# Seven block products for eight in half of the last batch's first product

## Chip, cores and metric

One core of a Trainium2 chip. The metric is the device time of one execution in microseconds (us). The engines are TensorE (PE, with its weight loads PEld), VectorE (DVE), ScalarE (ACT), GpSimd (POOL) and SyncE (SP, which here issues DMAs). Each runs its own queue in order; an instruction that waits holds up those behind it on its engine.

## The reference

Two stages: a cross attention between x (8 batches, 8 heads, 512 rows, 64 columns) and a state of 32 rows, and a two-layer product with a leaky ReLU on the result, 544 rows a batch (512 of x, 32 of state).

```python
scores = scale * x @ state.T          # softmax over the 32 state rows
xread = softmax(scores) @ state
scores2 = scale * state @ x.T         # softmax over the 512 rows of x
sread = softmax(scores2) @ x
t = concatenate([xread, sread], axis=2)   # heads side by side: (4352, 512)
h = t @ w_in                          # (4352, 2048)
g = maximum(0.01 * h, h)
out = g @ w_out                       # (4352, 512)
```

## The kernel before

Everything is computed transposed and in bf16 with fp32 sums. For the x rows of a batch the attention read and the first product are joined: `a.M` (2 halves of 128 rows, 2048 columns) is state times w_in, `a.aT` (2 halves of 128 rows, 512 columns) the softmax. `ff1` (L369) computes one block j of 128 of the 2048 columns of h: two matmuls of 512 columns (L372), one for each half g, into a PSUM tile `ph` of which there are two, and a leaky ReLU on ACT (L377) into `hT[:, j, :]`.

The second product of batches 2 to 7 is done by `Batch` and `Fast` with the Strassen-Winograd scheme: hT and w_out are cut into 2 x 2 blocks and multiplied in seven block products, numbered 1, 2, 6, 5, 7, 3, 4 in their order, each of eight units m (`Fast.unit`, L557: two matmuls of 256 columns). It needs sums of hT blocks (`Fast.sums`, L546, on DVE), sums of w_out made once, and it alternates between two PSUM banks: products 1, 6, 7, 4 add up in one, 2, 5, 3 in the other. Between products the bank is copied or joined: ACT copies 1, 6, 5 and 7 (`save`, L566), POOL adds 7 to 5 (L627), DVE joins 2, 3 and 4 with a copy and so makes the output (L569), and SP stores it (L594).

The loop over b from 2 (L932) has 16 steps s for each batch. Step s does `ff1` for j = s, small work of the attention of the next batch, and then `fill(s)`: `PACE[s]` units of second products, first those left of the batch before (41 of them), then the batch's own first 15. Batch 7 has no next batch (`nxt is None`), so its steps hold instead: at s=1 the last block of M, at s=4 the first three sums of w_in blocks for the sread rows (`FastIn.w_sum` 0, 1, 2, L411, each 128x2048 on DVE), at s=8 batch 7's sread (L300, L307), at s=10 the fourth (`w_sum(3)`) and the four sums of sread columns (`x_sums`, L423), at s=12 sums of hT for its own second product.

After the loop the sread rows of all batches (256 columns) go through both products: `FastIn.product` (L425) is a Strassen-Winograd product of w_in with them, seven products for each of two halves r in four PSUM banks, with copies on ACT (L463) and DVE (L465), joins on DVE (L468), an addition on POOL (L471) and leaky ReLUs on ACT (L457). Units of batch 7's second product run between. The schedule is manual: each engine's queue has the order in which the program issues its instructions. Tile pools with a tag and a number of buffers set the waits: a new tile of a tag waits for the last reader of the buffer that it takes.

Of the kernel before, what the change touches and what calls it, by code (L numbers as in the profile page):

```python
# [9 lines left out]
P = 128  # L10
B, H, S, D = 8, 8, 512, 64
# [8 lines left out]
BF16 = mybir.dt.bfloat16  # L20
FP32 = mybir.dt.float32
AF = mybir.ActivationFunctionType
ALU = mybir.AluOpType
# [4 lines left out]
def kernel(  # L28
# [9 lines left out]
    nc = tc.nc  # L38
# [4 lines left out]
    att = ctx.enter_context(tc.tile_pool(name="att", bufs=2))  # L43
# [4 lines left out]
    psum = ctx.enter_context(tc.tile_pool(name="psum", bufs=2, space=bass.MemoryType.PSUM))  # L48
# [5 lines left out]
    VEC, SCA, POO = nc.vector.tensor_copy, nc.scalar.copy, nc.gpsimd.tensor_copy  # L54
# [40 lines left out]
    xs, xl = {}, {}  # L95
# [273 lines left out]
    def ff1(a, hT, j):  # L369
        ph = psum.tile([P, S], FP32, name="ph", tag="ph")  # L370
        for g in range(2):
            nc.tensor.matmul(  # L372
                ph[:], lhsT=a.M[:, g, P * j:P * (j + 1)],
                rhs=a.aT[:, g, :],
                start=(g == 0), stop=(g == 1),
            )
        nc.scalar.activation(out=hT[:, j, :], in_=ph[:], func=AF.Prelu, alpha=0.01)  # L377
# [12 lines left out]
    class FastIn:  # L390


        R = NK

        def __init__(self, hT):
            w = w_in_bf[:].rearrange("p (r k) (i f) -> p i r k f", r=2, i=2)
            self.W = {(i, r): w[:, i - 1, r - 1] for i in (1, 2) for r in (1, 2)}
            x = sr_t[:].rearrange("p (c b) (r k) n -> p r c k b n", r=2, c=2)
            self.X = {(r, c): x[:, r - 1, c - 1] for r in (1, 2) for c in (1, 2)}
            self.hT, self.S, self.T = hT, {}, {}  # L400
            self.bank, self.sv = [{}, {}], [None, None]
# [23 lines left out]
        def product(self, r, n):  # L425
            b = self.bank[r]
            if n in (1, 2):
                tag = ("ph", "ph") if r == 0 else ("big", "sc")
                b[n] = psum.tile([P, self.R, P], FP32, name="pf", tag=tag[n - 1], bufs=2 - r)[:]
            bank = b[n] = b[{1: 1, 6: 1, 7: 1, 4: 1, 2: 2, 5: 2, 3: 2}[n]]  # L430
            W, X = self.W, self.X
            lhs = {1: W[1, 1], 2: W[1, 2], 4: W[2, 2]}.get(n)
            if lhs is None:
                lhs = self.S[{3: 3, 5: 0, 6: 1, 7: 2}[n]]
            rhs = {1: X[1, 1], 2: X[2, 1], 3: X[2, 2]}.get(n)
            if rhs is None:
                rhs = self.T[{4: 3, 5: 0, 6: 1, 7: 2}[n]]
            for q in range(self.R):
                j = self.R * r + q
                for k in range(2):  # L440
                    nc.tensor.matmul(  # L441
                        bank[:, q, :], lhsT=lhs[:, k, P * j:P * (j + 1)], rhs=rhs[:, k],
                        start=(n in (1, 2, 5) and q == 0 and k == 0), stop=(k == 1),
                        skip_group_check=True,
                    )
            self.done(r, n, bank)

        def done(self, r, n, bank):
# [23 lines left out]
            elif n == 4:  # L472
                relu(1, 1, sv[5])
                relu(1, 0, flat)

    class Y:
        pass

# [46 lines left out]
    class Fast:  # L525
# [9 lines left out]
        def sums(self, n, m0=0, m1=NM, eng=None):  # L535
            A, S = self.A, self.S
            if n not in S:
                pool, tag, bufs = self.homes[n]
                S[n] = pool.tile([P, NM, self.q], BF16, name=f"su{n}", tag=tag, bufs=bufs)
            u, v, op = (  # L540
                (A[2, 1], A[2, 2], ALU.subtract), (S[0], A[1, 1], ALU.subtract),
                (A[2, 1], A[1, 1], ALU.subtract), (A[1, 2], S.get(1), ALU.add),
            )[n]
            ms = slice(m0, m1)
            with nc.allow_low_precision(reason="operands of a product"):
                (eng or nc.vector).tensor_tensor(out=S[n][:, ms], in0=u[:, ms], in1=v[:, ms], op=op)  # L546
# [93 lines left out]
    PACE = (1, 4, 4, 4, 3, 4, 4, 3, 4, 4, 4, 4, 3, 4, 3, 3)  # L640
    PACE2 = (0,) * 10 + (3, 3, 2, 2, 2, 3)
# [137 lines left out]
    q = [recip0(0)]  # L779
# [47 lines left out]
    for j, tag in ((4, "py"), (6, "sc"), (8, "py"), (10, "ph"), (12, "py"), (14, "ph")):  # L827
        t, bk = open_ff1_0(tag)
# [67 lines left out]
    for s in range(16):  # L896
# [4 lines left out]
        if s % 2:  # L901
            pb, hT, i, jq = fill[s // 2]
# [29 lines left out]
    for b in range(2, B):  # L932
        hT = hpool.tile([P, 16, S], BF16, name="hT", tag="hT")
        a = att_of[b]
        nxt = att_of[b + 1] if b + 1 < B else None
        now = Batch(b, hT)
        std = []
        if b == 2:
            std = [(i, 3) for i in range(2)] + [(i, jq) for i in range(2, NT) for jq in range(4)]

        def fill(s):
            n = (PACE2 if b == 2 else PACE)[s]
            left = min(n, len(before.units)) if before else 0
            if left:
                before.run(left)
            if n > left:
                now.run(n - left)

        for s in range(16):
            if s == 11:  # L950
                fill(s)
            ff1(a, hT, s)
            if s == 0:
                if b + 2 < B:
                    load_x(b + 2, nc.sync)
                    open_xb(b + 2)
                a_a2t(a)
                if before:
                    for n in (0, 1):
                        before.f.sums(n, 4, 8)  # L960
            elif s == 1:
                if nxt is not None:
                    a_scores(nxt)
                m_evict(a, 3, a_m(a, 3, "big"), SCA)
                if b == 2:
                    a_sread_rows([a0])
                if nxt is not None:
                    a_shift(nxt)
                if b + 2 < B:
                    for h in range(0, H, 2):  # L970
                        cast_x(b + 2, h, h + 2, POO)
                if before:
                    before.f.sums(2, 4, 8)
            elif s == 3:
                if before:
                    before.f.sums(3)
                if nxt is not None:
                    a_max2(nxt)
                if b == 2:
                    weights_sum(0)  # L980
                    weights_sum(2)
            elif s == 4:
                if b == 2:
                    state_t(1)
                elif b == 4:
                    sread_t(0, 4)
                elif b == 7:
                    sread_t(1, 3)
            elif s == 8:
                if nxt is None:  # L990
                    a_sread(a)
                if b == 2:
                    weights_sum(1)
                    weights_sum(3)
            elif s == 12:
                for n in range(3):
                    now.f.sums(n, 0, 4)
            if nxt is None:
                if s == 4:
                    fi = FastIn(None)  # L1000
                    for n in range(3):
                        fi.w_sum(n)
                elif s == 10:
                    fi.w_sum(3)
                    fi.x_sums()
            if s == (9 if b == 2 else 7) and b + 2 < B:
                a_open(att_of[b + 2], b + 2)
                a_xt_dma(att_of[b + 2])
            if nxt is not None:
                if s == 5:  # L1010
                    a_exp(nxt)
                elif s in (7, 8):
                    a_exp2(nxt, s - 7)
                    if s == 7:
                        a_probs(nxt)
                elif s == 11:
                    a_probs2(nxt)
                elif s in (12, 13):
                    SCA(nxt.M[:, s - 12, DM:2 * DM], pm1[:, s - 12, :])
            if std:  # L1020
                i, jq = std.pop(0)
                piece(1, h1, i, jq)
            elif s != 11:
                fill(s)
            if s == 10 and nxt is not None:
                a_sread_rows([a1, a2] if b == 2 else [a])
                pm0 = a_m(nxt, 0, "big")
                pm1 = a_m(nxt, 1, "sc")
                pm2 = a_m(nxt, 2, "ph")
                for g, copy in enumerate((VEC, SCA)):  # L1030
                    copy(nxt.M[:, g, 2 * DM:3 * DM], pm2[g][:])
                m_evict(nxt, 0, pm0, SCA)
        before = now
# [24 lines left out]
    u, v = [psum.tile([P, 1, HC], FP32, name="yu", tag="ph")[:] for _ in range(2)]  # L1058
# [8 lines left out]
    for n in (1, 2, 6, 5, 7, 3, 4):  # L1067
        bank = v if n in (2, 5, 3) else u
# [6 lines left out]
        elif n == 7:  # L1075
            nc.gpsimd.tensor_tensor(
                out=ysb[1][:, :, HC:], in0=fs.sv[7][:], in1=fs.sv[5][:], op=ALU.add
# [46 lines left out]
```

## Time and profile before

| what | us |
|---|---|
| median of 3 runs (204.19 to 204.70) | 204.49 |
| profiled execution | 204.49 |
| its span | 202.7 |
| PE busy | 197.0 |
| DVE busy | 151.4 |
| ACT busy | 143.7 |
| POOL busy | 39.7 |

Batch 7's 16 steps lie from 157.72 to 177.66 of the span. In the steps 4 to 11, from 162.73 to 173.2, the groups that matter are (from the list of groups, the timeline and the answers by tile): `ph` matmuls of 512 columns, `yq` matmuls of 256, the leaky ReLU of 128x512 on ACT (604 ns), the copy of 128x512 on ACT (585 ns), the join on DVE (684 ns), the sums L411 of 128x2048 (1218 ns) and the addition on POOL (1266 ns). A mean duration runs from an instruction's start to its end; neighbours on one engine overlap somewhat, so the distance from start to start is the shorter figure where an engine is full.

```profile
161.56 1.22 DVE L411 TENSOR_TENSOR sw<-w_in_bf 128x2048 bf16<-128x2048 bf16 x1
...
162.82 1.23 DVE L411 TENSOR_TENSOR sw<-sw,w_in_bf 128x2048 bf16<-128x2048 bf16 x1
...
163.96 1.22 DVE L411 TENSOR_TENSOR sw<-w_in_bf 128x2048 bf16<-128x2048 bf16 x1
...
168.26 1.26 POOL L627 TENSOR_TENSOR yo<-sv,sv 128x512 f32<-128x512 f32 x1 [18.90 <-ACT sv L566]
...
170.43 0.69 DVE L569 TENSOR_TENSOR yo<-yq,sv 128x512 f32<-128x512 f32 x1 [5.25 <-PE yq L557]
171.03 1.22 DVE L411 TENSOR_TENSOR sw<-w_in_bf,sw 128x2048 bf16<-128x2048 bf16 x1
```

These lines of the timeline (start, duration, engine, line, operation, tiles, shapes, count, in brackets the idle time before it and who ended it) show DVE and POOL in that stretch: the three sums of w_in at s=4, DVE idle for 5.25 us before the join of batch 6's third product, and POOL's only work there, its addition at 168.26.

### The profile page before, as it was taken

To read this page: it belongs to the slowest core of one execution; us is meant where nothing else is said; L and a number is where in the kernel's file an instruction comes from. 1 tells how busy PE (TensorE), PEld (TensorE's weight loads), DVE (VectorE), ACT (ScalarE), POOL (GpSimd) and SP (SyncE) were. 2 spreads that over 40 slices of the span, in tenths; PEclk is the share of its full clock that TensorE was granted. 3 is DMA by queue.
4 is the path that set the end of the run, shared out by engine and by line. 5 is a ranking of instruction groups with operands and counts; after the bars stand their busy time and mean duration, and the time that the engine had idled before them with its cause. 6 is when DMAs were issued, how large, how long until landed. Compare 5 with 4: busy or idle time off the path is not lost.

```text
span 202.7 us, 4755 instructions
## 1 busy us (share of the span) xinstructions
PE 197.0 (97%) x1964; PEld 126.0 (62%) x1964; DVE 151.4 (75%) x230; ACT 143.7 (71%) x265; POOL 39.7 (20%) x66
## 2 busy tenths in 40 slices
PE   7899999999999999999999999999999999999993
PEld 2543544444344567766776767766767677799882
DVE  1677679599799969976996699769968853686612
ACT  3458848589869796978697878788778856467710
POOL 8831002021005005200251040200020002004250
PEclk9999999999999999999999999999999999999999
DMA  6999996999477895537946795250017100410035
GB/s 189 223 207 277 229 298 113 141 303 245 53 175 214 114 275 109 103 125 253 118 29 181 240 127 105 103 159 5 0 57 198 27 0 32 178 55 0 3 89 170
DMA packets 39733, 27.99 MB, mean 138 GB/s; under 512 B 25312, under 2 KB 36704, under 8 KB 39712
## 3 DMA queue, kind: packets, MB, share of 16 engines
q1 hardware_dynamic: 34512, 20.88, 44.6%
q0 software_dynamic: 4912, 6.55, 15.8%
q10 hardware_dynamic: 288, 0.26, 0.6%
q8 instruction: 15, 0.25, 0.5%
q14 instruction: 6, 0.05, 0.1%
HBM read 17.30 MB, written 8.91 MB: 129 GB/s over the span
## 4 chain that ended last, share of the span: by engine, by line
PE 96%; DVE 1%; ACT 1%; issue 0%
PE yq L557 36%; PE ph L372 23%; PE py L487 10%; PE pm L351 4%; PE pyw L487 3%; PE pf L441 3%; PE yu L557 3%; PE pspin L132 3%; PE ph L804 2%; PE sc L206 1%; PE psn L318 1%; PE phw L383 1%; PE php L804 1%; DVE M L365 1%; ACT xT L666 1%; PE scn L695 0%
## 5 line engine op out<-in xcount | busy, mean ns | idle before, releaser
L377 ACT ACTIVATE hT<-ph 128x512 bf16<-128x512 f32 x108 | 63.5, 604 | 22.0 <-PE ph L372 21.4
L372 PE MATMUL ph<-aT,M 128*128 128x512 bf16 x216 | 62.3, 379 | 0.0
L557 PEld LDWEIGHTS <-su 128*128 128x128 bf16 x416 | 39.7, 98 | 14.5 <-DVE su L546 1.7
L557 PEld LDWEIGHTS <-hT 128*128 128x128 bf16 x288 | 27.7, 98 | 11.7 <-issue 1.1
L557 PE MATMUL yq<-tw_xf,su 128*128 128x256 bf16 x192 | 27.2, 273 | 0.0
L105 POOL CAST xb<-xl 128x512 bf16<-128x512 f32 (+1 forms) x21 | 14.4, 724 | 65.2 <-PE ph L372 40.6
L557 PE MATMUL yq<-w_out_bf,hT 128*128 128x256 bf16 x192 | 27.0, 273 | 0.0
L372 PEld LDWEIGHTS <-M 128*128 128x128 bf16 x216 | 21.0, 98 | 9.3 <-issue 0.8
L546 DVE TENSOR_TENSOR su<-hT 128x1024 bf16<-128x1024 bf16 x24 | 16.8, 700 | 10.5 <-ACT hT L377 10.5
L487 PE MATMUL py<-w_out_bf,hT 128*128 128x512 bf16 x96 | 24.2, 379 | 0.0
L487 PEld LDWEIGHTS <-hT 128*128 128x128 bf16 x128 | 12.1, 98 | 14.6 <-issue 0.9
L627 POOL TENSOR_TENSOR yo<-sv,sv 128x512 f32<-128x512 f32 x6 | 7.8, 1300 | 54.1 <-ACT sv L566 42.7
L569 DVE TENSOR_TENSOR yo<-yq,sv 128x512 f32<-128x512 f32 x17 | 11.6, 685 | 6.5 <-PE yq L557 6.5
L566 ACT COPY sv<-yq 128x512 f32<-128x512 f32 x24 | 13.9, 585 | 2.0 <-PE yq L557 1.4
L365 ACT CAST M<-pm 128x1024 bf16<-128x1024 f32 x13 | 13.2, 1014 | 0.9 <-PE pm L351 0.8
L557 PE MATMUL yq<-w_out_bf,su 128*128 128x256 bf16 x96 | 13.1, 273 | 0.0
L557 PE MATMUL yq<-tw_x,su 128*128 128x256 bf16 x96 | 13.1, 272 | 0.0
L557 PE MATMUL yq<-tw_x,hT 128*128 128x256 bf16 x88 | 12.1, 273 | 0.0
L274 ACT ACTIVATE e<-sc,mcols 128x512 bf16<-128x512 f32 x16 | 11.1, 696 | 0.0
L216 DVE TRANSPOSE_TENSOR_REDUCE mrow<-sc 128x32 f32<-128x1024 f32 x7 | 8.7, 1245 | 2.4 <-PE sc L206 2.4
L266 DVE TENSOR_REDUCE mcol<-sc 128x2 f32<-128x1024 f32 x8 | 9.7, 1215 | 0.0
L247 DVE STREAM_TRANSPOSE qb<-qh 128x1024 bf16<-128x1024 bf16 x7 | 8.7, 1245 | 0.2
(147 smaller groups left out, 271.3 us busy)
## 6 DMA issues: line engine op xcount, KB each, us to landing
xl<-in_x_dram SPq DMA_DIRECT2D x5, 1024.0 KB, 7.1
out_dram<-yo SPq DMA_DIRECT2D x10, 512.0 KB, 3.0
w_in_bf<-in_moe_w_in_dram POOLq DMA_DIRECT2D x4, 512.0 KB, 9.1
w_out_bf<-in_moe_w_out_dram POOLq DMA_DIRECT2D x4, 512.0 KB, 17.0
out_dram<-ysb SPq DMA_DIRECT2D x8, 256.0 KB, 5.1
xf<-in_x_dram SPq DMA_DIRECT2D x2, 512.0 KB, 4.8
x<-in_x_dram POOLq DMA_DIRECT2D x2, 512.0 KB, 13.8
xl<-in_x_dram POOLq DMA_DIRECT2D x1, 1024.0 KB, 19.8
```

The lines of the kernel that those rows point to most:

```text
L105: copy(xs[b][:, :, h0:h1].rearrange("p t h d -> p h t d"), xl[b][:, h0:h1].rearrange("p h (t d) -> p h t d", t=NT),)
L216: nc.vector.tensor_reduce(out=m1[:], in_=flat.rearrange("p (c j) -> p c j", j=NS), axis=AX.X, op=ALU.max, apply_transpose=True,)
L266: nc.vector.tensor_reduce(out=m2[:], in_=a.sc[:], axis=AX.X, op=ALU.max, negate=True)
L274: nc.scalar.activation(out=a.e2[:, g], in_=a.sc[:, g, :], func=AF.Exp, bias=a.m2s[:, g:g + 1], scale=SCALE, accum_out=a.r2[:, g:g + 1],)
L365: copy(a.M[:, :, cols], pm[:])
L372: nc.tensor.matmul(ph[:], lhsT=a.M[:, g, P * j:P * (j + 1)], rhs=a.aT[:, g, :], start=(g == 0), stop=(g == 1),)
L377: nc.scalar.activation(out=hT[:, j, :], in_=ph[:], func=AF.Prelu, alpha=0.01)
L487: nc.tensor.matmul(y.py, lhsT=hT[:, j, P * i:P * (i + 1)], rhs=w_out_bf[:, j, :], start=(j == 0), stop=(j == 15),)
L546: (eng or nc.vector).tensor_tensor(out=S[n][:, ms], in0=u[:, ms], in1=v[:, ms], op=op)
L557: nc.tensor.matmul(bank[:, i, :], lhsT=lhs[:, m, P * i:P * (i + 1)], rhs=rhs[:, m, :], start=(first and m == 0 and (i == 0 or of is not No ...
L566: copy(t[:], bank)
L569: nc.vector.tensor_tensor(out=dst, in0=bank, in1=self.sv[n][:], op=ALU.add)
```

## The change

For batch 7 the blocks j = 0-3 and 8-11 of the first product are computed by a Strassen-Winograd product: M's column blocks 0-3 (i=1) and 8-11 (i=2), its halves g, and aT's halves g with their columns cut in two (c) make 2 x 2 blocks. A new class `FastLast` does it in two rounds r, each for two blocks j of both groups: seven products of two 256-column matmuls, in the order 1, 2, 6, 5, 7, 3, 4, in two banks of the tag `ph`. Each round has three copies on ACT (products 1, 6, 7), one on DVE (5), two joins on DVE (2, 3), one addition on POOL (7 and 5) and four leaky ReLUs on ACT, three of them from SBUF. Eight sums on DVE, four of 128x512 (M) and four of 128x256 (aT), are made at s=1.

Steps 0-3 of batch 7 now do j = 4-7, steps 4-11 the fourteen products (two a step, one at s=7 and at s=11) with the units of `PACE` spread behind each, steps 12-15 j = 12-15. The sums of w_in move from s=4 and 10 to s=6 (0 and 2), 10 (1) and 11 (3), still on DVE; `x_sums` moves from s=10 to s=13.

```diff
+    class FastLast:
+        R, Q = 2, S // 2
+        ORDER = [(r, n) for r in range(2) for n in (1, 2, 6, 5, 7, 3, 4)]
...
+        def sums(self):
...
+            ws = att.tile([P, 4, 4 * P], BF16, name="lw", tag="sh", bufs=1)
+            xs = att.tile([P, 4, self.Q], BF16, name="lx", tag="e1", bufs=1)
...
+                for n in (0, 2, 1, 3):
...
+                        nc.vector.tensor_tensor(out=d, in0=u, in1=v, op=op)
+
+        def product(self):
+            r, n = self.todo.pop(0)
+            R, Q = self.R, self.Q
+            if n == 1:
+                self.bank = {
+                    k: psum.tile([P, R, Q], FP32, name="pl", tag="ph")[:] for k in (1, 2)
+                }
...
+            bank, sv = self.bank[2 if n in (2, 5, 3) else 1], self.sv
...
+            for q in range(R):
+                j = R * r + q
+                nc.tensor.matmul(
+                    bank[:, q, :], lhsT=lhs[:, P * j:P * (j + 1)], rhs=rhs,
+                    start=(n in (1, 2, 5) and q == 0), stop=True, skip_group_check=True,
+                )
...
+            if n in (1, 6, 7):
+                SCA(sv[n], flat)
+                self.flush()
+            elif n == 5:
+                VEC(sv[n], flat)
+            if n in (2, 3):
+                k = {2: 1, 3: 6}[n]
+                nc.vector.tensor_tensor(out=sv[k], in0=flat, in1=sv[k], op=ALU.add)
+                self.late.append((relu, 0, n - 2, sv[k]))
+            elif n == 7:
+                nc.gpsimd.tensor_tensor(out=sv[5], in0=sv[7], in1=sv[5], op=ALU.add)
+            elif n == 4:
+                relu(1, 0, flat)
+                self.flush()
+                self.late.append((relu, 1, 1, sv[5]))
...
         for s in range(16):
-            if s == 11:
+            fast = nxt is None and 4 <= s < 12
+            if fast:
+                n = 1 if s in (7, 11) else 2
+                k = PACE[s]
+                for i in range(n):
+                    fl.product()
+                    units((i + 1) * k // n - i * k // n)
+            elif s == 11:
                 fill(s)
-            ff1(a, hT, s)
+            if not fast:
+                ff1(a, hT, 4 + s if nxt is None and s < 4 else s)
...
             if nxt is None:
-                if s == 4:
+                if s == 1:
+                    fl = FastLast(a, hT)
+                    fl.sums()
                     fi = FastIn(None)
-                    for n in range(3):
+                elif s in (6, 10, 11):
+                    for n in {6: (0, 2), 10: (1,), 11: (3,)}[s]:
                         fi.w_sum(n)
-                elif s == 10:
-                    fi.w_sum(3)
+                elif s == 13:
+                    fl.flush()
                     fi.x_sums()
...
-            elif s != 11:
+            elif s != 11 and not fast:
                 fill(s)
```

`flush` issues the leaky ReLUs kept in `late`, so that they stand behind the next copy on ACT.

## The prediction

> **What bounds the kernel now.** I read the page's engine shares first, then the chain that ended last, then the timeline of the last batch. TensorE (PE) is busy nearly all the span and carries the chain:
>
> ```profile
> PE 197.0 (97%) x1964; PEld 126.0 (62%) x1964; DVE 151.4 (75%) x230; ACT 143.7 (71%) x265; POOL 39.7 (20%) x66
> ...
> PE 96%; DVE 1%; ACT 1%; issue 0%
> ```
>
> The timeline (start, duration, engine, line, tiles, count, and in brackets the idle time before it) follows, in three pieces: what VectorE (DVE) does while GpSimd (POOL) works, twice in earlier batches, and one step s of the last batch:
>
> ```profile
> 86.31 0.69 DVE L248 TENSOR_TENSOR aT<-e,qb 128x1024 bf16<-128x1024 bf16 x1
> ...
> 148.10 1.27 POOL L627 TENSOR_TENSOR yo<-sv,sv 128x512 f32<-128x512 f32 x1 [19.78 <-ACT sv L566]
> ...
> 148.70 1.22 DVE L248 TENSOR_TENSOR aT<-e,qb 128x1024 bf16<-128x1024 bf16 x1
> ```
>
> ```profile
> 99.89 3.74 POOL L105 CAST xb<-xl 128x512 bf16<-128x512 f32 x4 [13.73 <-DMA xl<-in_x_dram]
> ...
> 100.38 0.68 DVE L546 TENSOR_TENSOR su<-hT 128x1024 bf16<-128x1024 bf16 x1
> 100.97 1.63 DVE L546 TENSOR_TENSOR su<-hT,su 128x2048 bf16<-128x2048 bf16 x1
> ```
>
> ```profile
> 161.43 0.59 PE L372 MATMUL ph<-aT,M 128*128 128x512 bf16 x2
> ...
> 161.86 1.04 PE L557 MATMUL yq<-tw_xf,su 128*128 128x256 bf16 x8
> ...
> 162.73 0.59 PE L372 MATMUL ph<-aT,M 128*128 128x512 bf16 x2
> ```
>
> The last piece: 161.43 to 162.73 is 1.30 us for two matmuls of 512 columns and eight of 256, thus 0.218 and 0.109 each; nothing but streaming. Any wait that PE gets here goes straight into the time, and any column saved comes straight out. The first: a DVE instruction with both inputs in SBUF takes 0.69 alone and 1.22 when it meets a POOL addition; it ends at 149.92, 0.55 after POOL's end at 149.37, so it stood still for the rest. The second: the 128x2048 sum, 1.22 alone, took 1.63, and POOL's four casts 3.74 for 2.29 elsewhere (62.57): POOL got in between two DVE sums that were queued back to back. DVE operations with one input in PSUM are not slowed (L468, two in 1.36 from 185.57, beside POOL's L471).
>
> **What the change takes away.** j 0-3 and 8-11 of batch 7 cost 16 matmuls of 512 columns, 16 x 0.218 = 3.49 us. They become 14 products of two 256-column matmuls, 28 x 0.109 = 3.05. Gain 0.44 us, 0.2% of the span: all there is to win. The order of the instructions as built confirms it: 24 more rows on PE, 12 loads and 12 matmuls. A load of 128 columns (98 ns) still lies under a 109 ns matmul.
>
> **What it adds.** I lay out the queues with these rows: a product's result can be read 0.38 after its start (two 256-column matmuls, 0.38) plus 0.04; ACT takes 0.60 for 128x512, 0.49 back to back from PSUM (two in 1.05-1.09), 0.61 from SBUF; DVE 0.68, or 0.60 back to back (L468, two in 1.28); PE restarts 0.06 after its releaser (L674 at 7.61 after ACT's end at 7.55). s=0-3 have the same PE work as before, so product 1 of round one starts at 162.73, where j=4 did. P1 to P7 below carry the code's numbers, in its order 1 2 6 5 7 3 4.
>
> Round one. P1 162.73, P2 163.17, P6 163.82 (its bank is free at 163.80: ACT's copy 163.15-163.74). P5 could start at 164.47, but its bank waits for DVE's addition of P2, and that stands behind the eight new sums and the sum L546 of 2048. DVE reaches the eight at 160.43. Four of 128x512 and four of 128x256: back to back 0.35 (su<-hs) and 0.21 (tx, 172.17), thus 2.2; at their full durations 0.42 and 0.29, thus 2.8. Then 1.13 to 1.22 for the 2048 and 0.68 for the addition: P5 at 164.54 to 165.23. A wait of 0.07 to 0.76; most are independent of the one ahead, so I take 0.20, near the low end. Then P5 164.67, P7 165.32, P3 165.98, P4 166.63.
>
> Between the rounds. DVE's addition of P3 is 166.40-167.08; behind it stand two w_in sums (L411, 1.22 each), moved from s=4, where POOL was idle, to here. ACT's copy of P7 ends 166.33, so POOL adds it to P5's copy at 166.37-167.63 (1.26). Both inputs of L411 lie in SBUF, so the first w_in sum stands still until 167.63 and ends 1.08 later (1.22 less the 0.14 that the blocked aT had already done), at 168.71. Meanwhile ACT does two leaky ReLUs from 167.05 and the copy of batch 6's product 7, which ends 168.74; then POOL's next addition (L627) asks, at 168.78. The second w_in sum is at the door at 168.71. By 0.07 us DVE is first: sum 168.71-169.85, addition of P2 of round two to 170.50, P5 of round two at 170.56. PE was there at 169.93 (P1 167.50, P2 168.15, the sread's 0.47, P6 169.28). Wait 0.60; bounds 0 (no collision) to 1.9 (below).
>
> One rule bears on this. The Trainium skill, "SBUF — State Buffer", section "Who interferes with whom", says that a VectorE instruction with two SBUF inputs and a GpSimd one that reads SBUF exclude each other, and whoever issues first keeps the port to its end. The aT rows agree (1.22 for 0.69). By it whether L627 or the second sum issues first is what decides the size, which the first rival below prices from rows.
>
> ACT gets six copies more in the eight steps (6 x 0.49 = 2.9). In round two its copy of P1 stands behind L627's input copy and ends 169.23, where P6 wants the bank at 169.28: between 0 and 0.2 in all, I take 0.10. The two rounds exchange their banks, so P1 and P2 of round two wait for nothing (bank free at 167.08, wanted 167.50).
>
> The tail. DVE comes out of the last step late: third w_in sum after P3 of round two, held by POOL again (172.25-173.50) to 174.6, batch 6's join to 175.2 (its bank is wanted at 175.35: no wait, 0.1 to spare), fourth sum 176.3, three L546 sums 178.2, four tx sums (1.05) 179.25. The loop then ends at 178.18, so DVE is 1.07 behind its end; in the trace of before it started its next sum 0.28 after it (177.94 against 177.66). So L468, 2.81 after the loop's end before, comes at 3.6. ACT's two ReLUs (0.61 each) and its copy of the sixth product follow, to 6.1; PE wants that bank for the seventh product 5.86 after the loop's end (183.52). Wait 0.3; had L468 slipped no more than 0.5 it would be hidden. Bounds 0 to 0.5, I take 0.35. No transfer is added; the stores of batch 6 leave later, with nothing behind them that ends the run.
>
> **Sum:** -0.44 + 0.20 + 0.10 + 0.60 + 0.35 = +0.81 us. The profiled execution took 204.49, its span 202.7 and 1.8 around it, and 204.49 is also the median of the runs: 205.3.
>
> **Rivals.**
> 1. POOL first. If L627 asks 0.1 us earlier, or the first w_in sum ends 0.1 later, POOL slips in as its cast did at 100.97: 168.7-170.0, second sum to 171.1, addition 171.73, P5 at 171.8. That is 1.25 more than above: 206.6. For it: 0.07 us decides. Against: in my layout DVE is ahead, and L627 hangs on ACT's whole queue.
> 2. Not slower: the sums pass POOL unhindered. No row shows a 2048-wide sum of w_in beside a POOL addition in fp32; if it is not held, the two sums end at 169.28, the addition at 169.90, and P5 of round two waits 0.03; DVE is 0.6 earlier at the loop's end and the tail wait is hidden. -0.44 + 0.20 + 0.10 + 0.03 = -0.1: 204.4. Decides: P5's wait below 0.4. For it: the sums are L411's alone, and the one that met POOL's L627 so far was L248. Against it: the two slowed rows above, of both kinds of sum and of both kinds of POOL work.
> 3. The eight sums at their full durations: P5 of round one waits 0.76, 0.56 more, 205.9; the later waits keep their size, since everything behind shifts alike. The upper end of the forecast's own range.
>
> **How the numbers follow.** Forecast (with 3 as its end) 0.48, 204.9 to 206.0; POOL first 0.27; unhindered 0.20; anything else 0.05. Range 204.4 (the unhindered case) to 206.8 (POOL first with 0.2 for its tail), leaving out little above and the full gain of 204.05 below. About 0.3%, 0.6 us, is what a measurement can tell from no change: slower means above 205.1. That takes POOL first, some three quarters of the forecast's share and most of the rest: 0.68. Within 0.3%: the unhindered case and the lower end of the forecast, 0.29. Faster by 0.6 is more than the columns saved: 0.03.
>
> **What would show it.** (Line numbers are those of before.) In the profile after: L411 of the first w_in sum at about 1.7-1.8 instead of 1.22, with POOL's addition beside it; PE's longest idle in the stretch ahead of P5 of round two, released by DVE; a second, small one ahead of P5 of round one; one ahead of the seventh product of L441. L627 between the two w_in sums means rival 1. The forecast is wrong if L411 keeps 1.22, or if PE's waits sum to less than 0.5.

## The result and the profile after

| | before | after |
|---|---|---|
| median of the runs (6 each) | 204.57 | 206.72 |
| their range | 204.19 to 205.53 | 206.13 to 207.06 |
| ratio after to before, with its 95% interval | | 1.010 (1.0074 to 1.0126) |
| profiled execution | 204.49 | 206.13 |
| its span | 202.7 | 204.2 |
| from the first product of step 4 to the end of the loop | 15.04 | 16.51 |
| from there to the first matmul of the last product (tile `yz`) | 20.44 | 20.79 |

The kernel is 2.15 us slower. The profiled execution of after is the fastest of its six, 0.59 below their median, so its trace shows less than these 2.15. The last two rows are read off the timeline between starts of PE instructions (before: 162.73, 177.77, 198.21; after: 162.43, 178.94, 199.73). They leave out that the two executions reach step 4 some 0.3 us apart, which no edit explains, and are the sharper measure: +1.47 in the steps 4 to 15 and +0.35 behind them, +1.82 in all.

In after.py L529 is the matmul of the seven products, L536 their leaky ReLU, L542 and L545 their copies on ACT and DVE, L548 the joins of products 2 and 3, L551 the addition of 7 to 5 on POOL. Of the old lines, L546 is now L632, L557 L643, L566 L652, L569 L655 and POOL's L627 L713.

The page of after, its engine shares (busy time, share, count) and the head of the chain that ended last:

```profile
span 204.2 us, 4783 instructions
PE 195.3 (96%) x1952; PEld 126.8 (62%) x1976; DVE 158.9 (78%) x244; ACT 146.8 (72%) x271; POOL 42.9 (21%) x68
...
PE 89%; DVE 5%; ACT 2%; issue 2%; ACTq 0%; DVEq 0%
```

PE is busy for less time and the span is longer. The chain, which was PE for 96%, now runs through DVE for 5%: PE waits for DVE. What PE waited for in after (line waiting, line waited for, total, times, longest):

```profile
PE pl L529 <- DVE ls L548: 1.7, 1, 1.7
...
PE pf L441 <- ACT sf L463: 0.2, 1, 0.2
```

Of the new code it is one wait, and one more in the tail. The stretch between the two rounds, in the timeline of after (start, duration, engine, line, tiles, count, in brackets the idle time before and who ended it):

```profile
164.21 0.38 PE L529 MATMUL pl<-lx,lw 128*128 128x256 bf16 x2
...
166.10 1.27 POOL L551 TENSOR_TENSOR ls<-ls 128x512 f32<-128x512 f32 x1 [17.03 <-ACT ls L542]
...
166.62 4.05 DVE L411 TENSOR_TENSOR sw<-w_in_bf 128x2048 bf16<-128x2048 bf16 x2
...
167.60 0.58 ACT L652 COPY sv<-yq 128x512 f32<-128x512 f32 x1
...
168.31 1.27 POOL L713 TENSOR_TENSOR yo<-sv,sv 128x512 f32<-128x512 f32 x1 [0.95 <-POOL ls L551]
...
169.04 0.60 PE L643 MATMUL yq<-w_out_bf,su 128*128 128x256 bf16 x4
...
170.59 0.68 DVE L548 TENSOR_TENSOR ls<-pl,ls 128x512 f32<-128x512 f32 x1
...
171.32 0.38 PE L529 MATMUL pl<-lx,lw 128*128 128x256 bf16 x2 [1.68 <-DVE ls L548]
```

The two sums of w_in, 1.22 each when alone, take 4.05 together. Each by itself, in the answer for line L411 of after (count, then the shortest, the median and the longest in ns, first and last start):

```profile
L411 DVE TENSOR_TENSOR sw<-w_in_bf x2: 1832/2064/2295, 166.6 to 168.4; 128x2048 bf16<-128x2048 bf16 x2
```

The first took 1.83 and so ran from 166.62 to 168.45, held by POOL's L551, which ended at 167.37. The second took 2.30, thus from 168.37 to 170.67, held by L713 to 169.58, with 1.09 to go. L713 started at 168.31: it asked 0.06 before the second sum. The addition of P2 stands behind that sum, and P5 of round two (171.32) behind the addition. PE was there at 169.04 + 4 x 0.109 = 169.48, so it waited 1.84 (the bracket, 1.68, counts from the modelled end of the last matmul). P5 of round one, the first line, waited 0.03: 164.18 to 164.21.

The tail, in the timeline of after behind the loop's end at 178.94:

```profile
180.04 0.68 DVE L632 TENSOR_TENSOR su<-hT 128x1024 bf16<-128x1024 bf16 x1
...
182.57 1.28 DVE L468 TENSOR_TENSOR sf<-pf,sf 128x512 f32<-128x512 f32 x2
...
184.42 1.05 ACT L463 COPY sf<-pf 128x512 f32<-128x512 f32 x2
...
185.04 0.61 PE L441 MATMUL pf<-tx,sw 128*128 128x128 bf16 x8 [0.18 <-ACT sf L463]
```

DVE starts its next sum 1.10 behind the loop's end, L468 comes at 3.63, ACT's copy follows late, and PE starts the product that needs its bank 6.10 after the loop's end (185.04 - 178.94), against 183.52 - 177.77 = 5.75 before: 0.35, all of what the tail adds. The two lines of before:

```profile
177.77 0.61 PE L441 MATMUL pf<-sr_t,w_in_bf 128*128 128x128 bf16 x8
...
183.52 0.61 PE L441 MATMUL pf<-tx,sw 128*128 128x128 bf16 x8
```

### The profile page after: what moved, and what is told of

Same layout as the page of the kernel before. It is cut to its first block, busy times and chain, and to the rows that moved or that the text cites. A ratio compares the mean times of both kernels' runs of the same rounds, so it can differ in the third digit from the quotient of the medians.

```text
span 204.2 us, 4783 instructions
## 1 busy us (share of the span) xinstructions
PE 195.3 (96%) x1952; PEld 126.8 (62%) x1976; DVE 158.9 (78%) x244; ACT 146.8 (72%) x271; POOL 42.9 (21%) x68
## 4 chain that ended last, share of the span: by engine, by line
PE 89%; DVE 5%; ACT 2%; issue 2%; ACTq 0%; DVEq 0%
PE yq L643 34%; PE ph L372 20%; PE py L573 10%; PE pm L351 4%; PE pyw L573 3%; PE yu L643 3%; PE ph L890 2%; PE pspin L132 2%; PE pf L441 2%; DVE sw L411 1%; PE sc L206 1%; PE psn L318 1%; PE php L890 1%; PE phw L383 1%; PE pl L529 1%
## 5 line engine op out<-in xcount | busy, mean ns | idle before, releaser
L377 ACT ACTIVATE hT<-ph 128x512 bf16<-128x512 f32 x100 | 58.9, 605 | 16.3 <-PE ph L372 13.9
L372 PE MATMUL ph<-aT,M 128*128 128x512 bf16 x184 | 55.1, 379 | 0.3
L643 PEld LDWEIGHTS <-su 128*128 128x128 bf16 x416 | 39.7, 98 | 13.5 <-DVE su L632 1.7
L643 PEld LDWEIGHTS <-hT 128*128 128x128 bf16 x288 | 27.7, 98 | 11.5 <-issue 1.1
L105 POOL CAST xb<-xl 128x512 bf16<-128x512 f32 (+1 forms) x21 | 14.9, 747 | 65.9 <-PE ph L372 29.5
L643 PE MATMUL yq<-tw_xf,su 128*128 128x256 bf16 x192 | 27.4, 273 | 0.3
L643 PE MATMUL yq<-w_out_bf,hT 128*128 128x256 bf16 x192 | 27.0, 273 | 0.1
L372 PEld LDWEIGHTS <-M 128*128 128x128 bf16 x200 | 19.4, 98 | 8.9 <-issue 1.0
L632 DVE TENSOR_TENSOR su<-hT 128x1024 bf16<-128x1024 bf16 x24 | 16.9, 705 | 8.4 <-ACT hT L377 8.4
L652 ACT COPY sv<-yq 128x512 f32<-128x512 f32 x24 | 13.9, 584 | 2.0 <-PE yq L643 1.4
L713 POOL TENSOR_TENSOR yo<-sv,sv 128x512 f32<-128x512 f32 x6 | 7.8, 1303 | 34.7 <-ACT sv L652 23.9
L643 PE MATMUL yq<-w_out_bf,su 128*128 128x256 bf16 x96 | 13.3, 273 | 0.2
L643 PE MATMUL yq<-tw_x,su 128*128 128x256 bf16 x96 | 13.4, 273 | 0.0
L655 DVE TENSOR_TENSOR yo<-yq,sv 128x512 f32<-128x512 f32 x17 | 11.6, 684 | 1.3 <-PE yq L643 1.3
L643 PE MATMUL yq<-tw_x,hT 128*128 128x256 bf16 x88 | 12.4, 273 | 0.0
```

The costliest lines, as they stand in the source:

```text
L105: copy(xs[b][:, :, h0:h1].rearrange("p t h d -> p h t d"), xl[b][:, h0:h1].rearrange("p h (t d) -> p h t d", t=NT),)
L372: nc.tensor.matmul(ph[:], lhsT=a.M[:, g, P * j:P * (j + 1)], rhs=a.aT[:, g, :], start=(g == 0), stop=(g == 1),)
L643: nc.tensor.matmul(bank[:, i, :], lhsT=lhs[:, m, P * i:P * (i + 1)], rhs=rhs[:, m, :], start=(first and m == 0 and (i == 0 or of is not No ...
L652: copy(t[:], bank)
L655: nc.vector.tensor_tensor(out=dst, in0=bank, in1=self.sv[n][:], op=ALU.add)
```

## The experiments

The theory: the w_in sums between the rounds are held by POOL's two additions, through what they share for reading SBUF, and the second hold comes from L713 slipping in between the two sums. Rivals: the sums themselves (2 x 1.22 on DVE's queue) make the wait, whoever works beside them; the place of the sums is not the cause but the seven products' own chain of copies and joins; the loss lies outside steps 4 to 15. All kernels start from the changed kernel, but for e6. They ran on three chips, each group beside the kernel before: e1, e2, e3 and e5 (before: 204.41), e4, e7 and e6 (before: 204.65), e8 and e9 (before: 204.34). The last column is read off the traces, like the two ahead of it.

| run | median | ratio to before (95%) | step 4 to loop end | to `yz` | both, against before |
|---|---|---|---|---|---|
| before | | | 15.04 | 20.44 | |
| after | 206.72 | 1.0100 (1.0074 to 1.0126) | 16.51 | 20.79 | +1.82 |
| e1 | 205.40 | 1.0042 (1.0030 to 1.0054) | 15.43 | 20.80 | +0.75 |
| e2 | 204.56 | 1.0008 (0.9995 to 1.0020) | 14.90 | 20.71 | +0.13 |
| e3 | 205.25 | 1.0041 (1.0028 to 1.0055) | 15.43 | 20.78 | +0.73 |
| e4 | 204.84 | 1.0013 (1.0001 to 1.0026) | 14.90 | 20.69 | +0.11 |
| e5 | 208.92 | 1.0199 (1.0156 to 1.0242) | 19.37 | 20.45 | +4.34 |
| e6 | 204.62 | 1.0000 (0.9990 to 1.0011) | 15.04 | 20.44 | 0.00 |
| e7 | 204.78 | 1.0016 (1.0004 to 1.0029) | 14.90 | 20.45 | -0.13 |
| e8 | 204.37 | 0.9994 (0.9984 to 1.0005) | 14.86 | 20.45 | -0.17 |
| e9 (e7 again) | 204.25 | 0.9992 (0.9982 to 1.0003) | 14.90 | 20.45 | -0.13 |

### e1 and e2: take POOL's reading away

```diff
 e1 and e2, Batch.done, n == 7:
-                nc.gpsimd.tensor_tensor(
-                    out=self.yo(1)[:, :, HC:], in0=f.sv[7][:], in1=f.sv[5][:], op=ALU.add
-                )
+                if self.b == B - 2:
+                    nc.gpsimd.memset(self.yo(1)[:, :, HC:], 0.0)
+                else:
+                    nc.gpsimd.tensor_tensor(...)
 e2 alone, FastLast.product, n == 7:
+                if r == 0:
+                    nc.gpsimd.memset(sv[5], 0.0)
+                else:
+                    nc.gpsimd.tensor_tensor(out=sv[5], in0=sv[7], in1=sv[5], op=ALU.add)
```

Both leave additions out, and with them a part of the result.

> The changed kernel, but POOL's addition of batch 6 (product 7 and 5, right half of its second rows) is replaced by a memset of the same tile: POOL writes but reads nothing, and that part of the output is zero. Theory (DVE's w_in sums and POOL's additions shut each other out): the first w_in sum is still held by POOL's addition of round one (about 1.8 us), the second runs in 1.22 instead of 2.30; PE's wait ahead of P5 of round two falls from 1.85 to about 0.7, the time by about 1.15 to 205.5. Rival (the two sums and the queue alone make the wait, whatever POOL does): second sum and wait unchanged, 206.7.

> As the run before, and POOL's addition of round one is a memset too (those blocks of h and what follows from them are not the reference's). Theory: both w_in sums take 1.22, DVE's addition of P2 of round two ends near 169.6, PE's wait ahead of P5 of round two is 0.1 to 0.2; the tail wait goes too because DVE is later by less; 204.8 to 205.0. Rival: waits as in the changed kernel, 206.7.

The answers for line L411, e1 and then e2:

```profile
L411 DVE TENSOR_TENSOR sw<-w_in_bf x2: 1212/1523/1834, 166.5 to 168.3; 128x2048 bf16<-128x2048 bf16 x2
```

```profile
L411 DVE TENSOR_TENSOR sw<-w_in_bf x2: 1218/1218/1219, 166.8 to 167.9; 128x2048 bf16<-128x2048 bf16 x2
```

Each addition taken from POOL gives one sum its 1.22 back, and only that one: 1.83 and 1.21 in e1, 1.22 twice in e2. PE's wait ahead of P5 of round two falls from 1.84 to 0.76 and to 0.14. The sums are as long, as many and in the same place in all three, so it is POOL's work beside them and not their own length. In e1 a POOL instruction still ran beside the first sum, and the sum was no longer than in after (1834 against 1832 ns), with L551 alone to hold it:

```profile
166.03 1.27 POOL L551 TENSOR_TENSOR ls<-ls 128x512 f32<-128x512 f32 x1 [17.03 <-ACT ls L542]
...
166.55 2.97 DVE L411 TENSOR_TENSOR sw<-w_in_bf 128x2048 bf16<-128x2048 bf16 x2
...
167.23 0.53 POOL L714 MEMSET yo<- 128x512 f32 x1
```

In this piece of e1's timeline the MEMSET, which only writes, runs 167.23 to 167.76 inside the sum of 166.55 to 168.38. The Trainium skill, "SBUF — State Buffer", section "Who interferes with whom", says that a VectorE instruction with two SBUF inputs contends with a GpSimd instruction that reads SBUF, not with one that only writes it; this row agrees. In e2 both memsets had ended (166.51) before the sums began, so e2 shows the absence of POOL and not its writing. The tail of e2 kept 0.27 that were expected to go: the third sum was still held (1.59) by round two's addition.

### e3: L713 made later, nothing left out

```diff
-        def done(self, n, bank):
+        def done(self, n, bank, late=False):
...
+            if n == 7 and self.b == B - 2 and not late:
+                self.kept = bank
+                return
...
                     fl.product()
+                    if s == 8 and i == 0:
+                        before.done(7, before.kept, late=True)
```

> The changed kernel with nothing left out; ACT's copy of batch 6's product 7 is issued behind its copy of P1 of round two, so POOL's addition L713 asks about 0.5 us later, after the second w_in sum has begun. Theory (who asks first keeps the port): DVE's second sum goes first and takes 1.22, POOL's addition waits for it and stands behind the sum in the timeline; PE's wait ahead of P5 of round two 0.7, time about 1.15 below the changed kernel, 205.5. Rival (POOL wins whenever it comes, or the collision is not the cause): the wait stays at 1.85 or grows by the 0.5 that POOL is later, 206.7 to 207.2.

ACT's copy of batch 6's product 7, and with it L713 (here L716), comes behind P1 of round two. The timeline of e3:

```profile
166.47 2.97 DVE L411 TENSOR_TENSOR sw<-w_in_bf 128x2048 bf16<-128x2048 bf16 x2
...
169.18 1.39 POOL L716 TENSOR_TENSOR yo<-sv,sv 128x512 f32<-128x512 f32 x1 [1.96 <-DVE sw L411]
169.36 0.68 DVE L548 TENSOR_TENSOR ls<-pl,ls 128x512 f32<-128x512 f32 x1
...
170.10 0.38 PE L529 MATMUL pl<-lx,lw 128*128 128x256 bf16 x2 [0.60 <-DVE ls L548]
```

This is the layout of the forecast: the first sum held, the second one (168.23 to 169.44, 1.21) first at the door, POOL behind it. L716 started 0.13 after the end of its copy on ACT (169.05), as L713 does in after (168.18 and 168.31), with 0.26 of the sum to go, and took 1.39 for 1.27. P5 of round two waits 0.76, as it does in e1, and the kernel takes 205.25, where the forecast was 205.3. The order of two instructions on two engines that came to the same place 0.06 us apart is worth 1.09 us of the 1.82.

### e4 and e7: the sums away from POOL

```diff
 e4 (e7: sums 1 at s == 6 and 3 at s == 10)
-                    fi = FastIn(None)
-                elif s in (6, 10, 11):
-                    for n in {6: (0, 2), 10: (1,), 11: (3,)}[s]:
-                        fi.w_sum(n)
+                elif s in (10, 11):
+                    fi.w_sum({10: 1, 11: 3}[s])
...
+            if b == B - 2 and s in (9, 13):
+                if s == 9:
+                    fi = FastIn(None)
+                fi.w_sum({9: 0, 13: 2}[s])
```

> The changed kernel with its first two w_in sums issued in batch 6 (at s=9 and s=13, where DVE sat idle 1.45 and 1.69 us in the profile of before); the other two stay at s=10 and 11. Theory: nothing stands ahead of DVE's addition of P2 of round two, PE's wait ahead of P5 of round two goes (0 to 0.1), the third sum is still held by POOL (1.7) and the tail wait of 0.2 stays: -0.44 + 0.03 + 0.05 + 0.2 = -0.15 against before, 204.3. Rival (the seven products' copies on ACT and DVE wait anyway): PE waits of 0.5 or more remain in the two rounds, 204.7 or more. Rival (DVE's gaps in batch 6 are not free): the same waits appear in batch 6.

The sums moved to batch 6 are 0 and 2, those that stood between the rounds; there they take 1.21 and 1.22. No wait of L529 is left in the list. Steps 4 to 15 take 14.90, 0.14 less than before, and the tail keeps 0.25 of its 0.35, since the third sum (1.58, held by POOL's addition of round two) still makes DVE late there. The kernel came out 0.11 above before by the trace where 0.15 below was expected: PE waited 0.13 ahead of P7 and 0.10 ahead of P3 of round two, for which the expectation had 0.05 in all, and the tail kept 0.25 for 0.2.

> As the run before, and the third sum moves to s=6 (one sum between the rounds instead of two), the fourth to s=10. Theory: the one sum is held by POOL's addition of round one (1.8), ends near 168.4, and DVE's addition of P2 still comes in time, so no wait ahead of P5; DVE ends the loop about 1.1 us earlier, so the tail wait of 0.2 goes too: -0.44 + 0.1 = -0.35 against before, 204.1, below both kernels. Rival (a single held sum is enough to make P5 wait): 0.3 or more ahead of P5 of round two, 204.4 or more.

In e7 one sum is back between the rounds. Its timeline there:

```profile
166.12 1.27 POOL L551 TENSOR_TENSOR ls<-ls 128x512 f32<-128x512 f32 x1 [17.03 <-ACT ls L542]
...
166.64 1.83 DVE L411 TENSOR_TENSOR sw<-sw,w_in_bf 128x2048 bf16<-128x2048 bf16 x1
...
168.34 1.28 POOL L713 TENSOR_TENSOR yo<-sv,sv 128x512 f32<-128x512 f32 x1 [0.95 <-POOL ls L551]
168.72 0.69 DVE L548 TENSOR_TENSOR ls<-pl,ls 128x512 f32<-128x512 f32 x1 [0.26 <-ACT ls L542]
```

The sum is held as before (1.83) and L713 comes at the same time as in after (168.34), but the DVE instruction behind the sum has one input in PSUM and runs beside L713 in its plain 0.69. P5 follows at 169.50 without a wait, and the tail is that of before (20.45). So one held sum is covered. Two free ones cost 0.14 (e2), one held and one free 0.76 (e1, e3), two held 1.84. The trace of e7 is 0.13 below before, not the 0.35 expected; waits of 0.12 ahead of P7 and 0.10 ahead of P3 are left in round two.

### e6: the sums' new places alone

The kernel before, with w_in's sums at s=6, 10 and 11 and `x_sums` at s=13, in the changed kernel's way.

```diff
-                if s == 4:
+                if s == 1:
                     fi = FastIn(None)
-                    for n in range(3):
+                elif s in (6, 10, 11):
+                    for n in {6: (0, 2), 10: (1,), 11: (3,)}[s]:
                         fi.w_sum(n)
-                elif s == 10:
-                    fi.w_sum(3)
+                elif s == 13:
                     fi.x_sums()
```

> The other half of the change alone: the kernel before, first product as it was, with the w_in sums at s=6, 10 and 11 and the sums of sread columns at s=13. Theory (the sums hurt only where a product's bank waits behind them): no PE wait in the sixteen steps, at most 0.1 in the tail; 204.4 to 204.7, no difference. Rival (moving the sums costs by itself, through the tail or the store of batch 6): 205 or more.

Nothing: 204.62 against 204.65, and 0.00 in both stretches. But the timeline of e6 has the two sums of s=6 some five us earlier than in after:

```profile
161.66 2.36 DVE L411 TENSOR_TENSOR sw<-w_in_bf 128x2048 bf16<-128x2048 bf16 x2
```

With none of the seven products' additions and copies ahead of them in DVE's queue they run as soon as DVE is free, 4.35 us before POOL's L627 (168.37), and all four sums take 1.21 to 1.22. So e6 shows that the new places in the program cost nothing by themselves, in the steps and in the tail. It does not show what sums held by POOL would cost without the seven products: there they never met.

### e5: the sums' old places

```diff
-                elif s in (6, 10, 11):
-                    for n in {6: (0, 2), 10: (1,), 11: (3,)}[s]:
+                elif s in (4, 10):
+                    for n in {4: (0, 1, 2), 10: (3,)}[s]:
                         fi.w_sum(n)
```

> The seven products alone: the sums of w_in stand where they stood before (three at s=4, one at s=10). Theory: DVE's queue is what decides; the three sums now stand ahead of the copy of P5 of round one, so P3 of round one waits about 2.8 us, and P5 of round two about 0; the end of the loop has less DVE work and its tail wait of 0.2 goes: 206.72 + 2.8 - 1.85 - 0.2 = about 207.5. Rival (the wait belongs to the collision with POOL alone, so sums at the old place where POOL is idle cost nothing): 204.3 to 204.9.

Worse, 208.92. The timeline of e5:

```profile
164.26 1.22 DVE L411 TENSOR_TENSOR sw<-w_in_bf 128x2048 bf16<-128x2048 bf16 x1
...
165.51 1.23 DVE L411 TENSOR_TENSOR sw<-sw,w_in_bf 128x2048 bf16<-128x2048 bf16 x1
...
166.65 1.22 DVE L411 TENSOR_TENSOR sw<-w_in_bf 128x2048 bf16<-128x2048 bf16 x1
...
167.79 0.69 DVE L545 COPY ls<-pl 128x512 f32<-128x512 f32 x1
...
168.53 0.38 PE L529 MATMUL pl<-aT,lw 128*128 128x256 bf16 x2 [2.66 <-DVE ls L545]
```

Here three unhindered sums (1.22 each, POOL idle) stand ahead of DVE's copy of P5, and PE, free at 165.71 for P3, waits 2.82 for its bank. With 0.44 saved that makes +2.41 (2.82 + 0.03 - 0.44), but the stretch shows +4.33. Waits of 0.08 ahead of P7 and 0.15 ahead of P3 of round two are a small part of the rest; the larger is in the windows of e5 (busy time and counts of PE, PEld, DVE, ACT, POOL, then the granted TensorE clock, the DMA share and GB/s):

```profile
165.00:168.00 3.00, 0.87 (x8) 0.62 (x7) 2.97 (x4) 1.21 (x3) 0.00 (x0) 1.00 0.00 0
168.00:170.00 2.00, 1.47 (x13) 1.30 (x13) 1.16 (x2) 0.40 (x1) 1.27 (x1) 0.95 0.03 8
170.00:173.00 3.00, 3.00 (x18) 2.07 (x17) 0.69 (x1) 2.20 (x5) 1.26 (x1) 0.50 0.00 0
173.00:174.00 1.00, 1.00 (x22) 0.95 (x20) 0.00 (x0) 0.30 (x2) 0.00 (x0) 0.90 0.00 0
```

After the idle time TensorE ran at half its clock. It comes up again, below.

### e8 and e9: what is left of the saving

e8 is e7 with the two ACT copies of batch 7's sread set behind the copy of P6, and the units of step 9 dealt 1 and 3 instead of 2 and 2; e9 is e7 once more.

```diff
 e8 against e7
+                    if s == 9 and i == 0:
+                        srt()
-                    units((i + 1) * k // n - i * k // n)
+                    units((1, 3)[i] if s == 9 else (i + 1) * k // n - i * k // n)
```

> The run e7 with its two small remaining PE waits in round two (0.12 ahead of P7, released by ACT; 0.10 ahead of P3, released by DVE) taken away: ACT's two copies of the sread go behind its copy of P6, and of the four units at s=9 one instead of two stands ahead of P5, so that DVE copies P5 ahead of batch 6's join. Theory (PE's waits are all that is left of the difference): the sixteen steps of the last batch shrink by 0.2 against e7, from 19.91 to about 19.7 (20.05 in the kernel before, 19.61 with no wait at all); time 0.2 below e7, 204.3 to 204.6, level with the kernel before or just below. Rival (something outside these steps makes the kernels with the seven products 0.2 to 0.3 longer than the aligned traces say): the steps shrink, and the median stays at 204.6 or more.

> The run e7 once more, on the same chip and beside the same runs of the kernel before as e8. Theory: 0.1 us below the kernel before, as its trace aligned at the last batch's first step says. Rival (outside the steps): 0.1 to 0.3 above it, as in the first run.

e8 did away with the waits ahead of P7 and P3, but a new one of 0.19 came ahead of P5 (169.55 to 169.74), for DVE's addition of P2 (168.99 to 169.68): one unit fewer stands there to cover it. So the steps 4 to 15 shrank by 0.04 (14.90 to 14.86) and not by the 0.2 expected, and e8 says little about its theory.

e7 had come out 0.13 us above before in its median and 0.13 below in its trace; repeated, it is 0.09 below, with an interval that holds 1. So the repeat does not bear out a loss outside the steps that were looked at. e8 and e9 can't be told from before. By the traces they keep 0.17 and 0.13 us of the 0.44, which is less than such runs resolve: that a version beats the kernel before is not shown. That they beat the changed kernel is: the ratios of e4, e7, e8 and e9 to before end at 1.003, that of the changed kernel begins at 1.007.

## Why the prediction was right or wrong

**What bounds the kernel: right.** PE's stream sets the time, and the four numbers that add up are PE's: -0.44 + 0.03 + 1.84 + 0.35 = 1.78 of the 1.82 that the trace shows.

**The gain of 0.44: right to within 0.05.** No run shows it bare, but e7 does with its waits: 14.90 in the steps 4 to 15, of which 0.03, 0.12 and 0.10 are idle ahead of P5, P7 and P3. 15.04 - 0.44 = 14.60, and these make 14.85, 0.05 short of what was measured.

**P5 of round one, 0.20: too high.** It waited 0.03. The eight sums ran back to back at the low end of the bounds, 160.13 to 162.28, 2.15 us. The third rival (0.76) is out with it.

**Between the rounds, 0.60: the step that failed.** The text had it that L627 asks at 168.78, the second sum is at the door at 168.71, and "by 0.07 us DVE is first". POOL was first, by 0.06. This term alone took 1.24 more than its 0.60 (the text's own times, 170.56 less 169.93, make 0.63). The mechanism, the first sum's length (1.83, 1.7 to 1.8 foreseen) and what was left of the second after POOL's end (1.09, 1.08 foreseen) were right, and the first rival had the case in full: it put P5's wait at 1.87 and the time at 206.6; 1.84 and 206.72 came. The range held because this rival was in it; the forecast's own 204.9 to 206.0 did not. The wrong call was to give the larger chance to a lead of 0.07 us in a layout whose own terms were uncertain by more. One of these terms decided it, as far as the timeline tells: with P5's wait 0.17 shorter than assumed, PE's products and all that hangs on them (the copy L652 and L713 behind it) came 0.17 earlier than laid out, while ACT, back to back from 163.94, could not deliver the copy of P7 that much earlier; so L551, and with it the end of the first sum, kept its place. That ACT's queue was the cause was not tried by itself. That L713's place decides was: in e3, with L713 behind the second sum, the forecast's layout came, with a wait of 0.76 for the 0.60 and 205.25 for the 205.3.

**Who issues first: borne out.** In after L713 started 0.06 before the second sum, 0.14 before the listed end of the first, and the second sum ended only 1.09 after L713; in e3 the sum started first, kept its 1.21, and POOL's addition was the longer one (1.39 for 1.27). The Trainium skill, "SBUF — State Buffer", section "Who interferes with whom", says that the shared ports are an exclusive lock and that the issue order decides who blocks; both rows agree. Two sums back to back in DVE's queue are two instructions: POOL came in between them.

**ACT's six copies, 0.10: covered by the long wait.** The terms above leave 0.04 for all small waits together. In e7, where P5 does not wait, PE waits 0.12 ahead of P7 for ACT's copy of P6 (169.65 to 170.23): about the size laid out, one product further on than the text had it.

**The tail, 0.35: right, in place and size.** DVE 1.10 behind the loop's end (1.07 foreseen), L468 at 3.63 (3.6), the wait ahead of the foreseen product of L441, 0.35. e7, whose DVE comes out of the loop in time, does not have it.

**The unhindered case** is the one that e2 shows by taking POOL's reads away: 204.56, 0.15 above the kernel before beside it, where 0.1 below was worked out; its tail wait was not hidden. With POOL's additions in place both sums were held.

**The span of the change's worth.** The change could win 0.44 at most and laid 2 x 1.22 of DVE work where POOL was at work and PE waited on DVE's queue. What it lost is POOL's holds, 0.61 and 1.08 of them on the two sums: without these (e2) it is even.

## What to carry to other kernels

Where the order of two engines at a shared resource hangs on less than the sum of the layout's own errors, price both orders and give the larger chance to neither; an order that is worth 1 us is worth fixing in the program, as e3 does with one copy moved. Before DVE work with both inputs in SBUF is moved into a gap, look at what GpSimd does in it, and put an instruction with a PSUM input, or none, behind it: one held sum was covered, two in a row cost 1.84. A product with fewer columns on TensorE pays only as long as PE's waits for the engines that join its parts stay below what the columns give; here they took back more.

## What the runs showed of the hardware

In e5 the granted clock was 0.50 from 170.0 to 173.0, 0.95 in the two us before and 0.90 in the one behind: some 3.4 us at half rate (0.2 + 3.0 + 0.2), after PE had been idle for 2.82. PE came back at 168.53 at full clock; the clock fell at about 169.8 (170.0 less 0.2), some 1.3 us later. Two products lie 1.28 apart there (170.29 and 171.57), 0.65 in after. The 1.84 of idle time in after left the clock at 1.00. e5's four runs, with their mean clock over the span, were 208.88 (0.992), 209.29 (0.992), 208.95 (0.989) and 207.62 (1.000): the one whose mean clock shows no dip is 1.3 us below the median and nearest to what was expected without one. In no execution of the other runs, whose traces have no wait of PE there longer than 1.84, was the mean clock below 0.996; that the idle time set off the dip is inferred from this. In the trace, half rate for 3.4 us is 1.7 us of lost work, and with the two waits of 0.08 and 0.15 it makes up the 1.92 (4.33 - 2.41) that the long wait leaves over. The Trainium skill, "TensorE: Matmul & The Clock Gate", section "What's actually happening", has the clock fall to half after an idle window of about 3.4 us that runs freely, and rise after as long a busy one. The length of the dip and its coming and going from run to run agree with that; that 2.8 us of idle time were enough does not, if 3.4 is read as the idle time that it takes. So a wait of 2.8 us cost some 1.3 to 1.7 us beyond itself in three runs of four.
